# Maxima of the pooled scores of four heads in one reduction, with the last 32 queries scored in every row group

## The chip, the cores and the metric

One Trainium2 chip, one of its cores. The metric is the time of one execution in microseconds on the device, the median of several runs. The engines are TensorE (PE, with its weight loads as PEld), VectorE (DVE), ScalarE (ACT), GpSimd (POOL) and SyncE (SP, which here only issues transfers).

## What is computed

Attention over 4 batches, 8 heads, 576 positions of 64 numbers, then two mixer layers. The part around the change is the pooled attention:

```
q_d = q.reshape(B, H, Sd, factor, D).mean(axis=3)     # factor 4, Sd = 144; k_d, v_d alike
s = scale * q_d @ k_d^T;  s = s - max(s);  a = exp(s)
out_d = (a / (sum(a) + 1e-09)) @ v_d;  out_up = repeat(out_d, 4, axis=2)
...
x = out_up + out_local          # out_local: each position over its neighbours at |i - j| < 4
u = x + token mixing;  x = u + relu(u @ w_ch1) @ w_ch2;  then the second mixer (cos, sin)
```

Weights are given in 64-bit floats, q, k and v in 32-bit floats.

## The kernel before

The attention runs on **quads**: four heads of one batch, 8 quads in all, numbered 0 to 7 here in the order batch, half. Heads lie in two pairs (p) of two (j: partitions 0 to 63 and 64 to 127). For a quad `quad_front` adds four neighbours of q and k (`qa`, `qkd`, L343 and L344 on DVE), scores the pooled queries against the pooled keys on PE into the PSUM tile `sd` (L362 for the first 128 queries of each head, 32 rows at a time; L371 for the last 32, head 2j + p in row group 2j + p), takes the row maxima into `mxd` on DVE (L379 for the four blocks of 144 in all rows, L387 twice for the last 32 queries in 64 rows each), scales them (L389), exponentiates on ACT (`pd`, L394 and L399), transposes on PE (`pdt`, L403 and L408), copies on ACT (`pts`), multiplies with the values on PE (`od`, L417 to L425), divides on DVE (`ods`, L431) and writes the result to DRAM (L437, L440) to read it back repeated (`xu`, L443 and L446).

`pair_local` does the neighbour attention of one pair: scores `s` (L469, L471), maximum and difference on DVE (`mx` L482, `pbuf` L483), exp, transposes `pt` (L496), product `o` (L504), division on DVE (L512 to L515), and on POOL the sum with the pooled result, x = x + xu (L523). `token_mix` takes a quad's x through two products with hi and lo halves (`t`; `xl` L533, `h` L548, transposes L569). `channel_mix` of batch 0 uses `uh`/`ul` (L102), first products `c` by `mm3` (L105 to L107) with `g` (L237 on ACT, L238 on DVE), second products L247 to L250, and the sum `um` (L252 on DVE) that frees one of two PSUM banks.

Beside that, 64-bit weights are loaded (`raw`, L119, four buffers) and split (`converted`): ACT L127 and L129, a clamp on POOL (L130, every fifth of the first on DVE), DVE L135, L143, L148, L155, ACT L157, POOL L158, and a last sum L160. Up to about 260 us this is interleaved with attention and mixing; afterwards the channel layers of the remaining batches and the second mixer run, almost all of it PE work.

The order of the first stage comes in two steps. The table `ORDER` sets the order in which the program writes its steps (F a step of a quad, L of a pair, T of token mixing, C channel mixing, W, X and Y weights, P and V loads). A scheduler then places each instruction on its engine by its own estimate of when its inputs are ready. So a changed instruction can change the order of others on every engine. Each engine, and SP's issues, then run strictly in the order so fixed.

Of the kernel before, what the change touches and what calls it, by code (L numbers as in the profile page):

```python
# [12 lines left out]
F32 = mybir.dt.float32  # L13
# [5 lines left out]
AF = mybir.ActivationFunctionType  # L19
ALU = mybir.AluOpType  # L20
AX = mybir.AxisListType
# [20 lines left out]
SD = S // 4  # L42
# [20 lines left out]
def kernel(  # L63
# [19 lines left out]
    act, dve, pool, pe = nc.scalar, nc.vector, nc.gpsimd, nc.tensor  # L83
# [171 lines left out]
    with ExitStack() as actx:  # L255
        sb1 = actx.enter_context(tc.tile_pool(name="a1", bufs=1))
        sb2 = actx.enter_context(tc.tile_pool(name="a2", bufs=2))
# [6 lines left out]
        def wide(tag, name):  # L264
            if tag == "s" and spare is not None:
                return spare.tile([128, 2, 512], F32, tag="sp", name=name)
            return big.tile([128, 2, 512], F32, tag="big", name=name)
# [64 lines left out]
        def quad_front(b, hh):  # L332

            at = f"{b}_{hh}"
# [3 lines left out]
            qd, kd = qkd[:, :, 0], qkd[:, :, 1]  # L338
            for p in range(2):
# [11 lines left out]
                out=vl,  # L351
                in0=vs[:, 4:5, :].to_broadcast([128, 4, 65]),
                in1=diag.unsqueeze(2).to_broadcast([128, 4, 65]),
                op=ALU.mult,
# [3 lines left out]
            sd = wide("sd", f"sd_{at}")  # L358
            for p in range(2):
                for c in range(4):  # L360
                    for j in range(2):
                        pe.matmul(  # L362
                            sd[32 * c : 32 * c + 32, j, p * SD : (p + 1) * SD],
                            qd[64 * j : 64 * j + 64, p, 32 * c : 32 * c + 32],
                            kd[64 * j : 64 * j + 64, p, :],
                            start=True,
                            stop=True,
                        )
                for j in range(2):
                    c = 2 * j + p  # L370
                    pe.matmul(  # L371
                        sd[32 * c : 32 * c + 32, j, 2 * SD : 3 * SD],
                        qd[64 * j : 64 * j + 64, p, SD - 32 : SD],
                        kd[64 * j : 64 * j + 64, p, :],
                        start=True,
                        stop=True,
                    )
            mx = sb2.tile([128, 5], F32, tag="mxd", name=f"mxd_{at}")
            dve.tensor_reduce(  # L379
                out=mx[:, 0:4].rearrange("p (j a) -> p j a", j=2),  # L380
                in_=sd[:, :, 0 : 2 * SD].rearrange("p j (a n) -> p j a n", a=2),
                axis=AX.X,
                op=ALU.max,
            )
            for j in range(2):
                r = slice(64 * j, 64 * j + 64)
                dve.tensor_reduce(out=mx[r, 4:5], in_=sd[r, j, 2 * SD : 3 * SD], axis=AX.X, op=ALU.max)  # L387
            scale = 1.0 / (16.0 * math.sqrt(D))
            dve.tensor_scalar(out=mx, in0=mx, scalar1=-scale, scalar2=None, op0=ALU.mult)  # L389
            pd = sb1.tile([128, 5, SD], F32, tag="pd", name=f"pd_{at}")  # L390
            for j in range(2):
                for p in range(2):
                    i = 2 * j + p
                    act.activation(  # L394
                        pd[:, i, :], sd[:, j, p * SD : (p + 1) * SD], AF.Exp, scale=scale, bias=mx[:, i : i + 1]
                    )
            for j in range(2):
                r = slice(64 * j, 64 * j + 64)
                act.activation(pd[r, 4, :], sd[r, j, 2 * SD : 3 * SD], AF.Exp, scale=scale, bias=mx[r, 4:5])  # L399
            yield  # L400
            pt = wide("pd", f"pdt_{at}")
            for i in range(5):
# [2 lines left out]
            for o, i in ((128, 0), (256, 4)):  # L405
                for c in range(4):
                    out = pt[32 * c : 32 * c + 32, 1, o : o + 128]
# [184 lines left out]

        pairs = [(b, p4) for b in range(B) for p4 in range(4)]
        fronts = [quad_front(b, hh) for b in range(B) for hh in range(2)]
        locals_ = [pair_local(*p) for p in pairs]
        tokens = {}
# [213 lines left out]
    sb2 = ctx.enter_context(tc.tile_pool(name="c2p", bufs=2))  # L810
    op = ctx.enter_context(tc.tile_pool(name="op", bufs=3))
# [171 lines left out]
```

## Time and profile before

| | us |
|---|---|
| median of 3 runs | 760.28 (759.94 to 762.93) |
| profiled execution | 763.31, of which the span is 761.5 |
| PE busy | 713.3 |
| DVE busy | 475.8 |
| ACT busy | 316.7 |
| POOL busy | 264.9 |

The table covers the whole span, which has two parts of different kind, so the shares of the span say little; the views by stretch do. A row of a timeline gives the start, the duration, the engine, the line and the operation (written tile <- read tiles), and in brackets how long the engine had stood idle before it and what ended that.

### The profile page before, as it was taken

The numbers are of one execution on the slowest core, as the hardware profiler recorded it, in microseconds if no ns is written. First come the engines' busy times: TensorE is split into PE (matmuls) and PEld (weight loads), VectorE is DVE, ScalarE is ACT, GpSimd is POOL, SyncE is SP. The second block draws the span as 40 slices with busy tenths as digits, with TensorE's granted clock in tenths as the row PEclk, the third lists the DMA queues.
The fourth block names the chain that finished last, engine by engine and source line by source line (L and its number), as shares of the span: only waits on it lengthen the run. The fifth ranks groups of instructions, "written<-read, shape, count | busy, mean of one in ns | idle before, by whom it ended". The sixth has DMA issues, their size and how long they took to land.

```text
span 761.5 us, 19905 instructions
## 1 busy us (share of the span) xinstructions
PE 713.3 (94%) x8272; PEld 679.0 (89%) x8272; DVE 475.8 (62%) x1007; ACT 316.7 (42%) x756; POOL 264.9 (35%) x280
## 2 busy tenths in 40 slices
PE   6776968779999999999999999999999999999998
PEld 4555766678988899999999999999999999999998
DVE  3999999795345332489548866684674454554432
ACT  2654755643345322355234424352663353452310
POOL 1778788785111010177347746460000000000000
PEclk9776989979999999999999999999999999999999
DMA  9577584765544423558547857520000400300101
GB/s 286 176 235 200 180 279 129 247 207 164 191 127 127 126 88 124 195 178 260 194 149 230 281 188 254 192 77 32 32 1 2 132 1 1 125 1 2 63 1 64
DMA packets 58699, 105.50 MB, mean 139 GB/s; under 512 B 7920, under 2 KB 34672, under 8 KB 58608
## 3 DMA queue, kind: packets, MB, share of 16 engines
q1 hardware_dynamic: 58608, 104.22, 42.5%
q8 instruction: 65, 1.06, 0.6%
q14 instruction: 26, 0.21, 0.1%
HBM read 74.71 MB, written 29.49 MB: 137 GB/s over the span
## 4 chain that ended last, share of the span: by engine, by line
PE 73%; DVE 14%; DMA 5%; issue 3%; SPq 2%; POOL 1%; ACT 1%; DVEq 0%; POOLq 0%; ACTq 0%
PE c L105 6%; PE c L107 6%; PE c L106 6%; PE y L107 5%; PE y L105 5%; PE y L106 5%; PE c L724 5%; PE c L721 4%; PE c L720 4%; DVE ww L143 3%; PE th L105 2%; PE th L106 2%; PE th L107 2%; PE o L107 2%; PE o L105 2%
## 5 line engine op out<-in xcount | busy, mean ns | idle before, releaser
L130 POOL TENSOR_SCALAR ww<-ww 128x256 f32<-128x256 f32 (+1 forms) x85 | 99.7, 1175 | 117.5 <-ACT ww L129 88.7
L107 PE MATMUL y<-wrh,zl 128*128 128x288 f32 x256 | 75.7, 296 | 0.0
L106 PE MATMUL y<-wrl,zh 128*128 128x288 f32 x256 | 75.6, 295 | 0.0
L105 PE MATMUL y<-wrh,zh 128*128 128x288 f32 x256 | 75.6, 296 | 0.0
L707 ACT ACTIVATE g<-c 128x288 fp32r<-128x288 f32 x72 | 29.3, 412 | 90.6 <-PE c L107 90.6
L127 ACT ACTIVATE wf<-raw 128x256 bf16<-128x256 uint32 (+1 forms) x91 | 40.2, 442 | 38.8 <-DVE wrl L160 8.5
L143 DVE SCALAR_TENSOR_TENSOR ww<-raw,ww 128x256 uint32<-128x256 uint32 (+1 forms) x91 | 52.9, 583 | 2.2
L708 DVE SCALAR_TENSOR_TENSOR g<-c,g 128x288 fp32r<-128x288 f32 x72 | 32.3, 455 | 33.9 <-ACT g L707 33.4
L523 POOL TENSOR_TENSOR x<-x,xu 128x640 f32<-128x640 f32 x16 | 25.8, 1614 | 71.6 <-DVE x L515 40.4
L135 DVE TENSOR_SCALAR ww<-ww 128x256 uint32<-128x256 uint32 (+1 forms) x91 | 45.7, 504 | 4.2 <-POOL ww L130 4.0
L106 PEld LDWEIGHTS y<-wrl,zh 128*128 128x128 f32 x256 | 48.1, 188 | 0.0
L105 PEld LDWEIGHTS y<-wrh,zh 128*128 128x128 f32 x256 | 48.1, 188 | 0.0
L107 PEld LDWEIGHTS y<-wrh,zl 128*128 128x128 f32 x256 | 48.0, 188 | 0.0
L725 DVE TENSOR_TENSOR ut<-c,ut 128x288 f32<-128x288 f32 x48 | 21.9, 455 | 37.6 <-PE c L724 37.4
L148 DVE TENSOR_SCALAR we<-ww 128x256 uint16<-128x256 uint16 (+1 forms) x91 | 41.9, 462 | 0.7
L105 PE MATMUL th<-thh,cxh 128*128 128x256 f32 x144 | 41.1, 285 | 0.6 <-issue 0.6
L155 DVE TENSOR_TENSOR wf<-wf,we 128x256 bf16<-128x256 bf16 (+1 forms) x91 | 38.7, 426 | 3.5 <-ACT thh L157 0.5
L106 PE MATMUL th<-thl,cxh 128*128 128x256 f32 x144 | 40.7, 283 | 0.0
L107 PE MATMUL th<-thh,cxl 128*128 128x256 f32 x144 | 40.7, 283 | 0.0
L129 ACT ACTIVATE ww<-raw 128x256 f32<-128x256 f32 (+1 forms) x91 | 39.6, 435 | 0.0
L879 DVE TENSOR_TENSOR cx<-y,cx 128x288 f32<-128x288 f32 x32 | 14.6, 455 | 37.0 <-PE y L107 37.0
L106 PE MATMUL o<-cul,wch 128*128 128x288 f32 x128 | 37.4, 295 | 0.0
(285 smaller groups left out, 2468.8 us busy)
## 6 DMA issues: line engine op xcount, KB each, us to landing
raw<-w_ch SPq DMA_DIRECT2D x56, 256.0 KB, 3.3
qk<-qkT SPq DMA_DIRECT2D x16, 582.0 KB, 4.7
uh<-uh SPq DMA_DIRECT2D x16, 576.0 KB, 4.2
ul<-ul SPq DMA_DIRECT2D x16, 576.0 KB, 4.4
xT<-ut SPq DMA_DIRECT2D x14, 576.0 KB, 3.3
vw<-vloc SPq DMA_DIRECT2D x32, 219.4 KB, 4.2
vd<-vtok SPq DMA_DIRECT2D x8, 650.0 KB, 7.6
raw<-w_ri SPq DMA_DIRECT2D x18, 288.0 KB, 3.5
```

The costliest lines, as they stand in the source:

```text
L105: pe.matmul(out, lh, rh, start=start, stop=False)
L106: pe.matmul(out, lh, rl, start=False, stop=False)
L107: pe.matmul(out, ll, rh, start=False, stop=stop)
L127: act.activation(f, words[:, :, 0], AF.Copy, scale=2.0**-52)
L129: act.activation(w, high, AF.Abs)
L130: next(clamps).tensor_scalar(out=w, in0=w, scalar1=F64_LEAST, scalar2=F64_MOST, op0=ALU.max, op1=ALU.min)
L135: dve.tensor_scalar(out=wu, in0=wu, scalar1=3, scalar2=0x3FFFFFF8, op0=ALU.logical_shift_left, op1=ALU.bitwise_and,)
L143: dve.scalar_tensor_tensor(out=wu, in0=words[:, :, 1], scalar=0xC0000000, in1=wu, op0=ALU.bitwise_and, op1=ALU.bitwise_or)
L148: dve.tensor_scalar(out=e.bitcast(U16), in0=w.bitcast(U16).rearrange("p (n t) -> p n t", t=2)[:, :, 1], scalar1=0xFF80, scalar2=None, op0= ...
L155: dve.tensor_tensor(out=f, in0=f, in1=e, op=ALU.mult)
L708: dve.scalar_tensor_tensor(out=h2, in0=ps[:, 0:HALF], scalar=0.0, in1=h1.bitcast(F32), op0=ALU.max, op1=ALU.subtract)
L724: pe.matmul(ps[:, 0:HALF], w[cb // 2][2][:, cb % 2, d], hs[cb][1], start=False, stop=last_one)
```

## The change

The last 32 queries are scored in two row groups for each pair and half instead of one (L372: eight matmuls a quad instead of four), so that all 128 rows of the third block of `sd` hold scores of their half j. One reduction (L380) over both halves and three blocks gives six maxima a row in a tile of 2 x 3; it stands for three reductions. The scaling (L387) covers six columns instead of five, and the exponentials read their bias from the new places.

```diff
--- before.py
+++ after.py
@@ -366,37 +366,38 @@
                             start=True,
                             stop=True,
                         )
+
                 for j in range(2):
-                    c = 2 * j + p
-                    pe.matmul(
-                        sd[32 * c : 32 * c + 32, j, 2 * SD : 3 * SD],
-                        qd[64 * j : 64 * j + 64, p, SD - 32 : SD],
-                        kd[64 * j : 64 * j + 64, p, :],
-                        start=True,
-                        stop=True,
-                    )
-            mx = sb2.tile([128, 5], F32, tag="mxd", name=f"mxd_{at}")
+                    for c in (p, 2 + p):
+                        pe.matmul(
+                            sd[32 * c : 32 * c + 32, j, 2 * SD : 3 * SD],
+                            qd[64 * j : 64 * j + 64, p, SD - 32 : SD],
+                            kd[64 * j : 64 * j + 64, p, :],
+                            start=True,
+                            stop=True,
+                        )
+            mx = sb2.tile([128, 2, 3], F32, tag="mxd", name=f"mxd_{at}")
             dve.tensor_reduce(
-                out=mx[:, 0:4].rearrange("p (j a) -> p j a", j=2),
-                in_=sd[:, :, 0 : 2 * SD].rearrange("p j (a n) -> p j a n", a=2),
+                out=mx,
+                in_=sd[:, :, 0 : 3 * SD].rearrange("p j (a n) -> p j a n", a=3),
                 axis=AX.X,
                 op=ALU.max,
             )
-            for j in range(2):
-                r = slice(64 * j, 64 * j + 64)
-                dve.tensor_reduce(out=mx[r, 4:5], in_=sd[r, j, 2 * SD : 3 * SD], axis=AX.X, op=ALU.max)
             scale = 1.0 / (16.0 * math.sqrt(D))
             dve.tensor_scalar(out=mx, in0=mx, scalar1=-scale, scalar2=None, op0=ALU.mult)
             pd = sb1.tile([128, 5, SD], F32, tag="pd", name=f"pd_{at}")
             for j in range(2):
                 for p in range(2):
-                    i = 2 * j + p
                     act.activation(
-                        pd[:, i, :], sd[:, j, p * SD : (p + 1) * SD], AF.Exp, scale=scale, bias=mx[:, i : i + 1]
+                        pd[:, 2 * j + p, :],
+                        sd[:, j, p * SD : (p + 1) * SD],
+                        AF.Exp,
+                        scale=scale,
+                        bias=mx[:, j, p : p + 1],
                     )
             for j in range(2):
                 r = slice(64 * j, 64 * j + 64)
-                act.activation(pd[r, 4, :], sd[r, j, 2 * SD : 3 * SD], AF.Exp, scale=scale, bias=mx[r, 4:5])
+                act.activation(pd[r, 4, :], sd[r, j, 2 * SD : 3 * SD], AF.Exp, scale=scale, bias=mx[r, j, 2:3])
             yield
             pt = wide("pd", f"pdt_{at}")
             for i in range(5):
```

The number of instructions changes on PE (32 matmuls more) and on DVE (16 reductions fewer). The order changes on all engines in the first stage, up to row 3220 of PE's 6686 and row 419 of DVE's 1009; behind that it is the same.

On DVE, ahead of the `h` by which quad 3's token mixing passes from its first product to its second. Before:

```order
L515 TENSOR_TENSOR x_0_2694<-o_0_2650,rl_0_2691 128x2x5x64
L135 TENSOR_SCALAR ww<-ww 128x256
L252 TENSOR_TENSOR um_0_1166<-c_0_0_0_0_0_3049,um_0_1166 128x288
L143 SCALAR_TENSOR_TENSOR ww<-raw,ww 128x256
L148 TENSOR_SCALAR we<-ww 128x256
L252 TENSOR_TENSOR um_0_1166<-c_0_0_0_0_1_3069,um_0_1166 128x288
L155 TENSOR_TENSOR wf<-wf,we 128x256
L135 TENSOR_SCALAR ww<-ww 128x256
L143 SCALAR_TENSOR_TENSOR ww<-raw,ww 128x256
L548 SCALAR_TENSOR_TENSOR h_1_1_0_2559<-t_1_1_0_2543,h_1_1_0_2558 128x256
```

Now:

```order
L135 TENSOR_SCALAR ww<-ww 128x256
L102 TENSOR_TENSOR ul_0_1_0_3143<-um_1_1171,uh_0_1_0_3142 128x288 x2
L143 SCALAR_TENSOR_TENSOR ww<-raw,ww 128x256
L102 TENSOR_TENSOR ul_0_1_0_3143<-um_1_1171,uh_0_1_0_3142 128x288 x2
L148 TENSOR_SCALAR we<-ww 128x256
L483 TENSOR_REDUCE mx_2_2778<-s_2_2735 128x10
L155 TENSOR_TENSOR wf<-wf,we 128x256
L135 TENSOR_SCALAR ww<-ww 128x256
L484 TENSOR_TENSOR pbuf_133<-s_2_2735,mx_2_2778 128x2x5x38
L549 SCALAR_TENSOR_TENSOR h_1_1_0_2569<-t_1_1_0_2553,h_1_1_0_2568 128x256
```

The two sums into `um`, which stood ahead of this `h`, are now behind it; `mx` and `pbuf` of the tenth pair, which stood behind it, are now ahead.

On PE, from the end of quad 3's first product to the transposes that open its second (`t_1_1_0_0`). Before:

```order
L107 MATMUL t_1_1_1_2576<-xh_1_2536,w1l 128x256
L543 MATMUL t_1_1_1_2576<-xh_1_2536,w1h 128x256
L544 MATMUL t_1_1_1_2576<-xs_1_2538,w1s 128x256
L469 LDWEIGHTS id_132
L469 MATMUL s_2_2723<-msk,id_132 128x190
L469 LDWEIGHTS id_132
L469 MATMUL s_2_2723<-msk,id_132 128x190
L471 MATMUL s_2_2723<-qk_2_2325 32x38 x13
L569 MATMUL t_1_1_0_0_2596<-idt,x_1_2216 128x128 x2
L105 MATMUL t_1_1_0_0_2596<-w2h,h_1_1_0_2558 128x256
```

Now (`c` is the second product of batch 0's channel mixing):

```order
L250 MATMUL c_0_0_0_0_0_3061<-g_0_0_0_0_2_3007,c21h 128x288
L250 MATMUL c_0_0_0_0_0_3061<-g_0_0_0_0_3_3024,c21h 128x288
L250 MATMUL c_0_0_0_0_0_3061<-g_0_0_0_0_4_3041,c22h 128x288
L250 MATMUL c_0_0_0_0_0_3061<-g_0_0_0_0_5_3058,c22h 128x288
L247 MATMUL c_0_0_0_0_1_3081<-g_0_0_0_0_0_2972,c20h 128x288
L248 MATMUL c_0_0_0_0_1_3081<-g_0_0_0_0_0_2972,c20l 128x288
L247 MATMUL c_0_0_0_0_1_3081<-g_0_0_0_0_1_2989,c20h 128x288
L248 MATMUL c_0_0_0_0_1_3081<-g_0_0_0_0_1_2989,c20l 128x288
L570 MATMUL t_1_1_0_0_2606<-idt,x_1_2224 128x128 x2
L105 MATMUL t_1_1_0_0_2606<-w2h,h_1_1_0_2568 128x256
L106 MATMUL t_1_1_0_0_2606<-w2l,h_1_1_0_2568 128x256
```

In all, 14 second products of channel mixing that stood ahead of the transposes now stand behind them, and 27 score matmuls of the tenth pair and all 42 of the eleventh pair (40 and 2 of the mask) now stand ahead; the 13 shown before belong to the tenth pair as well.

On POOL, around the first sum of quad 3's x with its pooled result. Before:

```order
L130 TENSOR_SCALAR ww<-ww 128x256
L160 TENSOR_TENSOR c12l<-ww,wf 128x256
L158 TENSOR_TENSOR ww<-ww,c22h 128x256
L523 TENSOR_TENSOR x_1_2216<-x_1_2216,xu_1_2160 128x640
L160 TENSOR_TENSOR c22l<-ww,wf 128x256
L130 TENSOR_SCALAR ww<-ww 128x256
```

Now:

```order
L346 TENSOR_TENSOR vd_1_2572<-vd_1_2572 128x650
L160 TENSOR_TENSOR c12l<-ww,wf 128x256
L130 TENSOR_SCALAR ww<-ww 128x256
L158 TENSOR_TENSOR ww<-ww,c22h 128x256
L130 TENSOR_SCALAR ww<-ww 128x256
L160 TENSOR_TENSOR c22l<-ww,wf 128x256
L158 TENSOR_TENSOR ww<-ww,c22h 128x256
L524 TENSOR_TENSOR x_1_2224<-x_1_2224,xu_1_2168 128x640
L130 TENSOR_SCALAR ww<-ww 128x256
```

The sum with `xu` now has ahead of it one clamp (`ww<-ww` L130), one `c22l`, one subtraction (L158) and one `vd` sum that stood behind it.

## Rows read from the trace of the kernel before

**Rows 1.** Busy us of each engine by stretch, count in brackets, granted clock, DMA.
```profile
core 0: us, PE busy (x) PEld busy (x) DVE busy (x) ACT busy (x) POOL busy (x), PEclk, DMA share, GB/s
20.00:130.00 110.00, 84.61 (x1811) 67.54 (x1810) 105.31 (x220) 63.43 (x170) 87.12 (x92) 0.82 0.63 198
130.00:140.00 10.00, 7.82 (x144) 6.88 (x144) 6.21 (x17) 5.21 (x17) 6.24 (x8) 1.00 0.87 268
140.00:168.00 28.00, 20.11 (x381) 18.03 (x381) 27.47 (x54) 16.69 (x46) 24.79 (x26) 0.88 0.66 206
168.00:172.00 4.00, 4.00 (x40) 3.51 (x41) 2.50 (x7) 0.86 (x3) 2.31 (x3) 0.63 0.61 234
168.00:761.50 593.50, 587.01 (x5682) 577.40 (x5682) 328.53 (x704) 226.50 (x516) 142.88 (x149) 1.00 0.36 117
```

**Rows 2.** Timeline of PE: two long waits of the first stage.
```profile
103.05 0.61 PE L105 MATMUL c<-uh,c10h 128*128 128x288 f32 x1 [4.37 <-DVE pbuf L483]
...
167.94 0.44 PE L569 MATMUL t<-idt,x 128*128 128x128 f32 x2 [3.07 <-DVE h L548]
```

**Rows 3.** DVE by line and shape, 0 to 245 us: count, busy us, mean ns.
```profile
L135 DVE TENSOR_SCALAR ww<-ww 128x256 uint32<-128x256 uint32 x37 | 21.2, 578 | 4.1 <-POOL ww L130 4.0
L155 DVE TENSOR_TENSOR wf<-wf,we 128x256 bf16<-128x256 bf16 x37 | 19.5, 528 | 0.5
L148 DVE TENSOR_SCALAR we<-ww 128x256 uint16<-128x256 uint16 x37 | 15.9, 435 | 0.4
...
L482 DVE TENSOR_REDUCE mx<-s 128x10 f32<-128x380 f32 x14 | 7.6, 544 | 11.2 <-PE s L471 11.1
L483 DVE TENSOR_TENSOR pbuf<-s,mx 128x380 f32<-128x380 f32 x14 | 7.6, 543 | 0.2
L379 DVE TENSOR_REDUCE mxd<-sd 128x4 f32<-128x576 f32 x8 | 5.9, 744 | 0.6 <-PE sd L371 0.5
...
L387 DVE TENSOR_REDUCE mxd<-sd 64x1 f32<-64x144 f32 x16 | 4.8, 299 | 0.1
...
L252 DVE TENSOR_TENSOR um<-c,um 128x288 f32<-128x288 f32 x8 | 3.6, 451 | 7.8 <-PE c L250 7.8
```

**Rows 4.** Timeline of PE: from one group's start to the next one's.
```profile
12.70 0.48 PE L362 MATMUL sd<-qkd 64*32 64x144 f32 x16 [2.54 <-DVE qkd L344]
...
13.36 1.80 PE L282 MATMUL s<-zero 128*128 128x320 bf16 x12
...
43.67 0.33 PE L469 MATMUL s<-msk,id 128*128 128x190 bf16 x2
...
44.76 0.65 PE L417 MATMUL od<-vl,pts 128*32 128x260 f32 x8
...
179.17 0.29 PE L247 MATMUL c<-g,c20h 128*128 128x288 f32 x1
...
181.55 0.71 PE L496 MATMUL pt<-idt,pbuf 128*128 128x128 f32 x5
```

**Rows 5.** Timelines of POOL and DVE: the gap near 136 us.
```profile
136.44 1.55 POOL L523 TENSOR_TENSOR x<-x,xu 128x640 f32<-128x640 f32 x1 [3.76 <-DMA xu<-od]
...
138.59 1.06 POOL L130 TENSOR_SCALAR ww<-ww 128x256 f32<-128x256 f32 x1
...
139.68 0.82 DVE L135 TENSOR_SCALAR ww<-ww 128x256 uint32<-128x256 uint32 x1 [3.41 <-POOL ww L130]
```

**Rows 6.** POOL by line and shape, 100 to 168 us: count, busy us, mean ns.
```profile
L130 POOL TENSOR_SCALAR ww<-ww 128x256 f32<-128x256 f32 x14 | 17.0, 1215 | 2.3 <-ACT ww L129 2.3
...
L160 POOL TENSOR_TENSOR c22l<-ww,wf 128x256 fp32r<-128x256 f32 x4 | 3.4, 865 | 0.0
L158 POOL TENSOR_TENSOR ww<-ww,c22h 128x256 f32<-128x256 f32 x4 | 3.3, 836 | 0.0
...
L346 POOL TENSOR_TENSOR vd<-vd 128x650 f32<-128x650 f32 x2 | 2.8, 1392 | 0.5 <-DVE ww L143 0.5
```

**Rows 7.** Timeline of SP: the issue of the two `vw` loads.
```profile
132.04 0.58 SPq L457 DMA_DIRECT2D vw<-vloc  x1
132.66 0.43 SPq L458 DMA_DIRECT2D vw<-vloc  x1
```

## Prediction

> **What bounds the kernel now.** I read the busy time by stretch first, because the shares of the whole span hide two regimes [rows 1]. From 168 us to the end PE is busy 587.01 of 593.50 us: there the kernel is as long as PE's work. Before that PE is busy only 84.61 + 7.82 + 20.11 of 148 us, so 35.5 us of PE are lost, and in the same stretches DVE is busy 105.31 of 110 and 27.47 of 28 us. DVE, which runs its instructions in order, sets the pace up to 168 us, apart from ten microseconds (130 to 140) where it is busy 6.21. The waits of PE say the same: its two long ones shown are 4.37 us ended by `pbuf` and 3.07 us ended by `h`, both DVE's [rows 2]. The second of these is the last long wait: at 167.94 PE opens the second product of quad 3's token mixing, and from there on it hardly stops. I take that point as the hinge. The end of the kernel is the moment at which DVE finishes this `h`, plus the PE work that stands behind the hinge in PE's order. A microsecond of DVE counts if it stands ahead of the `h`, a microsecond of PE counts if it stands behind the hinge; the rest lies in waits. The price of what the change removes is in [rows 3], of what it adds and moves on PE in [rows 4], and the hole in DVE's work near 136 us in [rows 5].
>
> **The change part by part.** *The reductions.* Per quad 744 + 2 x 299 = 1342 ns go [rows 3]. From 144 to 576 elements a row the reduction grows by 445 ns, 1.03 ns an element, which leaves 299 - 148 = 151 ns that each instruction costs whatever its size. The new one reads 864 elements: 864 x 1.03 + 151 = 1041 ns. It saves 0.30 us a quad, in effect the fixed part of two instructions, since the elements are as many as before (576 + 144 + 144). The ends: nothing saved, if it cost 1342, and 0.60 saved, if it cost the 744 of the present large one; I take 0.30, from the slope of the two rows. Six of the eight quads stand ahead of the `h`: -1.8 us (0 to -3.6).
>
> *The order on DVE ahead of the `h`.* Counting the instructions ahead of it before and now, apart from the reductions: two sums into `um` have gone behind it (2 x 451 ns = -0.9), and the tenth pair's `mx` and `pbuf` (544 + 543) and one more instruction each of L135, L148 and L155 (578 + 435 + 528) have come ahead: +2.63 [rows 3]. Together +1.7 us. The reductions' gain ahead of the hinge is thus nearly used up by what the scheduler put there: -0.1.
>
> *The order on PE behind the hinge.* Fourteen second products of channel mixing fall behind it. Eighteen of them take from 179.17 to 181.55, 0.132 us each, so +1.85. Score matmuls, 27 of the tenth pair and all 42 of the eleventh, have come ahead; a pair's 42 take from 43.67 to 44.76, so 69 are 1.79 us that no longer stand behind. Net +0.1 [rows 4].
>
> *The added matmuls.* Twenty records of `sd` (ten matmuls, two records each) take from 12.70 to 13.36, 0.033 us a record [rows 4]. Four matmuls more are eight records, 0.26 us a quad. Of the eight quads six stand ahead of the hinge, where PE has 35.5 us of waits to hide them; uncovered, they would cost 1.6 us. Two stand behind: +0.5 us (0 if they overlap with others, twice that at the lower clock). The reduction waits for `sd` as it did before; DVE's idle time ahead of it was 0.6 us in eight quads [rows 3], so the wait is rarely the last one.
>
> *The sixth column and the exponentials' bias* are at nothing: the scaling has one element more, the six exponentials are as many and as large, and ACT is busy 16.69 of 28 us in the last stretch ahead of the hinge [rows 1].
>
> *The gap near 136 us.* DVE stood idle 3.41 us because POOL's clamp came late, and the clamp was late because POOL, in order, stood 3.76 us at x = x + xu, whose transfer had not landed [rows 5]. In the new order one clamp, one `c22l`, one subtraction and one `vd` sum stand ahead of that sum: 1215 + 865 + 836 + 1392 ns = 4.3 us of work that POOL can do first [rows 6]. On SP two `vw` loads now go out ahead of the `xu` loads, which makes these later by 0.58 + 0.43 = 1.0 us [rows 7]. POOL's wait would be 3.76 - 4.3 + 1.0 = 0.5 us, and DVE gets a clamped block before it instead of after it. The full gain would be 3.4 us; it is nothing if the pulled-forward rows wait for their own inputs, which DVE itself delivers. I take -2.0, nearer the full gain, since `vd` needs no DVE and the clamp needs only a loaded block.
>
> The sum: -1.8 + 1.7 + 0.1 + 0.5 - 2.0 = -1.5 us on the profiled execution, whose span is 761.5 and time 763.31. That execution was 3.0 us above the median of 760.28; I apply the difference to the median: 758.8. Without the gap's gain the sum is +0.5, with all of it -2.9.
>
> Two rules of the Trainium skill bear on this. First, PE's clock: in the four microseconds behind the 3.07 us wait the granted clock is 0.63, so 1.2 GHz for most of them, against 2.4 GHz in nearly all that follows; that loses 4 x 0.37 = 1.5 us of PE [rows 1, 2]. The Trainium skill (TensorE: Matmul & The Clock Gate, Part 1) says that the throttled clock is PE's default and activity releases it; the trace agrees. By it, filling the wait would be worth more than the wait's end alone: PE now has most of `c`'s second product there, and the lost clock might come back, which makes a sum of -3.0 instead of -1.5; it is a part of the fast rival below. Second, POOL's clamp takes 1215 ns on average in a stretch where DVE is nearly always busy and 1.06 us at 138.59, when DVE waited [rows 5, 6]. The Trainium skill (GPSIMD Engine Reference, 1. Specifications) says that POOL shares its SBUF interfaces with DVE and that DVE instructions with two SBUF inputs contend with it. The removed reductions read PSUM, so by that rule taking them away gives POOL no relief, and the freed time fills with instructions that do contend. That speaks for the POOL rival.
>
> **The rivals.** *The gap stays* (the pulled-forward POOL rows wait in their turn): +0.5, so 760.8. For it: the gap is a chain over DMA, POOL and DVE, and only one link is mended. *POOL sets the pace* ahead of the hinge: it is busy 24.79 of 28 us there [rows 1]. Then neither the gap nor the -1.8 of the reductions counts: +2.3, so 762.6. Against it: DVE waited for a clamp only 4.1 us in 245 [rows 3], and most of that is the gap. *The filled hinge* (fast): the gap goes wholly, and PE, fed with `c` in place of the 3.07 us wait, keeps its clock: -0.1 + 0.1 + 0.5 - 3.4 - 1.5 = -4.4, so 755.9. Against it: PE work moved into a wait ahead of the hinge only helps where it isn't missed elsewhere. *A new PE wait behind the hinge* (slower): the sums into `um` free the two PSUM banks of channel mixing; they now stand behind the `h` among other DVE work, while 14 of the products that need them stand behind the hinge too. If PE, which follows strictly in order, reaches the next product before its bank is free, it waits. Its longest wait of the kind, a `c` held up by DVE, was 4.37 us [rows 2], and the half clock behind such a wait costs 1.5: -1.5 + 5.9 = +4.4, so 764.7. It decides if PE's waits between 168 and 190 us grow by more than 2 us. Against it: about ten microseconds of other PE work (`t` and scores) stand between.
>
> **How the numbers follow.** My forecast of 758.8 (its own range 756.9 to 760.8, from the gap's two ends) gets 0.45, the gap stays 0.15, POOL sets the pace 0.10, the filled hinge 0.15, a new wait 0.15. About 0.5% of 760.28, 3.8 us, is what a measurement of this kernel can tell from no change. Below 756.5 lie most of the filled hinge and a tail of the forecast, since the order changes on every engine and the sum prices only the differences around one hinge: 0.24. Above 764.1 lie most of the new wait, little of POOL's pace, and the like tail: 0.18. Between: 0.58. The range of 755.2 to 764.9 reaches to the fast and slow rivals and leaves out two in ten.
>
> **What would show it right or wrong.** The reduction's row should read about 1040 ns, eight times, and `sd`'s added records should leave PE's busy time behind the hinge longer by about half a microsecond. DVE's longest idle time between 130 and 145 us should be under 2 us, and POOL's wait for `xu` under 1.5. PE's last long wait should still end with an `h` of quad 3, near 166 to 167 us. The forecast is wrong if PE's last long wait has moved to another place, above all one behind 170 us, or if DVE's busy share ahead of 168 us has fallen below 90% outside the gap, since then the hinge was never DVE's to set.

## The result and the profile after

The changed kernel takes 770.53 us (four runs, 767.43 to 772.42) against 761.58 for the kernel before in the same session: 1.0107 times as long (95% interval 1.0080 to 1.0134). The forecast was 758.8. A profiled execution is one run out of a spread of several us: that of the changed kernel, 767.43, was its fastest, and that of the kernel before, 763.31, was slower than all four of its runs in that session. Spans therefore differ by 4.0 us where medians differ by 9.0. Here the ratios judge, and the traces only tell where.

The view by stretch after, columns as in [rows 1]:

```profile
20.00:130.00 110.00, 79.44 (x1771) 63.50 (x1772) 93.98 (x205) 59.88 (x161) 84.60 (x90) 0.84 0.67 201
130.00:140.00 10.00, 8.65 (x130) 7.06 (x129) 9.36 (x23) 5.96 (x19) 7.11 (x9) 0.67 0.70 220
140.00:168.00 28.00, 22.94 (x477) 20.15 (x476) 21.98 (x47) 17.05 (x47) 22.25 (x25) 0.80 0.59 160
168.00:172.00 4.00, 4.00 (x103) 3.43 (x103) 3.71 (x8) 2.07 (x7) 4.00 (x4) 0.93 0.97 276
168.00:765.50 597.50, 590.57 (x5694) 582.27 (x5693) 333.51 (x704) 226.67 (x519) 144.55 (x150) 1.00 0.36 118
```

DVE's column changes most. Ahead of 130 us it is idle 16.0 us instead of 4.7, and from 140 to 168 us 6.0 instead of 0.5. That is not the loss itself: PE's idle time from 20 to 168 us grows by only 1.5 us, from 35.5 to 37.0, and its granted clock is lower from 130 us on, 0.67 and 0.80 instead of 1.00 and 0.88. Behind 168 us PE lacks 6.9 us, as it lacked 6.5 before. The loss is ahead of the hinge.

The new reduction by line and shape, 0 to 250 us (count, busy us, mean ns), and the timeline of POOL and DVE around the old gap, which answers to [rows 5]:

```profile
L380 DVE TENSOR_REDUCE mxd<-sd 128x6 f32<-128x864 f32 x8 | 8.4, 1050 | 0.2 <-PE sd L372 0.2
```

```profile
140.84 1.54 POOL L524 TENSOR_TENSOR x<-x,xu 128x640 f32<-128x640 f32 x1 [0.29 <-ACT c22h L157]
...
141.14 0.55 DVE L483 TENSOR_REDUCE mx<-s 128x10 f32<-128x380 f32 x1 [1.57 <-PE s L472]
...
143.44 0.76 DVE L135 TENSOR_SCALAR ww<-ww 128x256 uint32<-128x256 uint32 x1 [1.16 <-POOL ww L130]
...
146.38 0.76 DVE L343 TENSOR_TENSOR qa<-qk 128x576 f32<-128x576 f32 x1 [1.30 <-DMA qk<-qkT]
```

The wait for `xu` is gone, as forecast, and three shorter waits of DVE, 4.0 us together, stand just behind. Quad 3's transposes, which waited 3.07 us at 167.94 [rows 2], now start without a wait, but at 174.01, six us later (PE's timeline):

```profile
161.82 0.50 PE L470 MATMUL s<-msk,id 128*128 128x190 bf16 x2 [2.17 <-DVE x L516]
...
174.01 0.38 PE L570 MATMUL t<-idt,x 128*128 128x128 f32 x2
```

From that point to the end of the span it is 591.5 us, against 593.6 before. So the hinge lost 6.1 us, and what stands behind it gained 2.1.

One place where four engines stand still one behind the other, in the timelines of POOL, ACT, DVE and PE after:

```profile
112.14 1.53 POOL L524 TENSOR_TENSOR x<-x,xu 128x640 f32<-128x640 f32 x1 [3.93 <-DVE we L148]
...
115.75 0.43 ACT L127 ACTIVATE wf<-raw 128x256 bf16<-128x256 uint32 x1 [4.04 <-POOL c21l L160]
...
116.97 0.46 DVE L238 SCALAR_TENSOR_TENSOR g<-c,g 128x288 fp32r<-128x288 f32 x1 [3.15 <-ACT g L237]
119.86 1.95 DVE L534 TENSOR_TENSOR xl<-x,xh 128x1280 fp32r<-128x1280 f32 x1 [2.43 <-ACT xh L533]
...
117.48 0.61 PE L105 MATMUL c<-uh,c11h 128*128 128x288 f32 x1 [3.18 <-DVE g L238]
```

POOL's sum of quad 2's x with `xu` stands early and waits, by the view for a row of DVE. Behind it in POOL's order are the weight rows that free ACT's next buffer; behind ACT's conversion is the `g` that DVE wants; and PE wants DVE's `g` for a free bank.

### The profile page after: what moved, and what is told of

Same layout as the page of the kernel before. It is cut to its first block, busy times and chain, and to the rows that moved or that the text cites. A ratio compares the mean times of both kernels' runs of the same rounds, so it can differ in the third digit from the quotient of the medians.

```text
span 765.5 us, 20014 instructions
## 1 busy us (share of the span) xinstructions
PE 715.8 (94%) x8336; PEld 682.4 (89%) x8336; DVE 466.5 (61%) x991; ACT 315.2 (41%) x756; POOL 262.7 (34%) x280
## 3 DMA queue, kind: packets, MB, share of 16 engines
q8 instruction: 65, 1.06, 0.6%
## 4 chain that ended last, share of the span: by engine, by line
PE 75%; DVE 8%; DMA 6%; POOL 4%; issue 3%; ACT 2%; SPq 1%; POOLq 0%; DVEq 0%; ACTq 0%
PE c L105 6%; PE c L107 6%; PE c L106 6%; PE y L107 5%; PE y L105 5%; PE y L106 5%; PE c L725 4%; PE c L722 4%; PE c L721 4%; DMA vw<-vloc 2%; PE th L105 2%; PE th L106 2%; PE th L107 2%; PE o L107 2%; PE o L105 2%
## 5 line engine op out<-in xcount | busy, mean ns | idle before, releaser
L130 POOL TENSOR_SCALAR ww<-ww 128x256 f32<-128x256 f32 (+1 forms) x85 | 99.1, 1169 | 115.7 <-ACT ww L129 89.5
L135 DVE TENSOR_SCALAR ww<-ww 128x256 uint32<-128x256 uint32 (+1 forms) x91 | 43.4, 478 | 7.9 <-POOL ww L130 7.7
L148 DVE TENSOR_SCALAR we<-ww 128x256 uint16<-128x256 uint16 (+1 forms) x91 | 41.7, 460 | 0.6
L107 PE MATMUL o<-cuh,wcl 128*128 128x288 f32 x128 | 37.4, 295 | 0.0
```

The costliest lines, as they stand in the source:

```text
L107: pe.matmul(out, ll, rh, start=False, stop=stop)
L130: next(clamps).tensor_scalar(out=w, in0=w, scalar1=F64_LEAST, scalar2=F64_MOST, op0=ALU.max, op1=ALU.min)
L135: dve.tensor_scalar(out=wu, in0=wu, scalar1=3, scalar2=0x3FFFFFF8, op0=ALU.logical_shift_left, op1=ALU.bitwise_and,)
L148: dve.tensor_scalar(out=e.bitcast(U16), in0=w.bitcast(U16).rearrange("p (n t) -> p n t", t=2)[:, :, 1], scalar1=0xFF80, scalar2=None, op0= ...
```

## The experiments

In most of them each engine is held to a list of instructions, by edges that fix the order of issue and make no instruction wait for another's end:

```diff
+    for text in RANKS.values():     # one list per engine
...
+        for earlier, later in zip(row, row[1:]):
+            tc.add_manual_dep(traced[int(later)], traced[int(earlier)].name, info, reason="order")
```

A "lag" is worked out from two traces: instruction by instruction the start minus the start in the kernel before, and of these the median over VectorE's rows that the kernel before begins in a given ten us. The table has each ratio to the kernel before, and VectorE's busy time between 113 and 130 us, a stretch that the experiments single out.

| kernel | ratio (95%) | DVE busy of 17 us |
|---|---|---|
| before | 1 | 16.90 |
| changed | 1.0107 (1.0080 to 1.0134) | 11.33 |
| e1 changed instructions, old order | 1.0045 (1.0025 to 1.0066) | 14.89 |
| e2 old instructions, new order | 1.0110 (1.0092 to 1.0128) | 11.68 |
| e3 added matmuls, own order | 1.0160 (1.0128 to 1.0192) | 15.65 |
| e4 one reduction, own order | 1.0196 (1.0165 to 1.0227) | 16.11 |
| e5 new order to 97 us, then old | 1.0042 (1.0023 to 1.0062) | 16.68 |
| e6 old order to 97 us, then new | 1.0106 (1.0079 to 1.0133) | 8.90 |
| e7 one GpSimd row later | 1.0095 (1.0069 to 1.0122) | 11.26 |
| e8 added matmuls, old order | 1.0055 (1.0036 to 1.0075) | 16.90 |
| e9 one reduction, old order | 0.9987 (0.9973 to 1.0001) | 16.86 |
| e10 new order, old in 97 to 128 us | 1.0067 (1.0046 to 1.0088) | 16.62 |
| e11 old order, new in 97 to 128 us | 1.0101 (1.0080 to 1.0121) | 6.56 |
| e12 tail scores made twice, old order | 1.0021 (1.0008 to 1.0034) | 16.68 |
| e13 chain undone in the changed kernel | 1.0105 (1.0069 to 1.0140) | 7.60 |
| e14 chain undone in e11 | 1.0100 (1.0072 to 1.0129) | 9.75 |
| e15 added matmuls, last two quads | 1.0003 (0.9985 to 1.0021) | 16.90 |
| e16 e14 with weight rows put back | 1.0129 (1.0100 to 1.0158) | 7.27 |
| e17 e11 with weight rows put back | 1.0138 (1.0109 to 1.0167) | 5.75 |
| e18 as e16, in the changed kernel | 1.0121 (1.0088 to 1.0153) | 6.19 |

**Order or instructions: e1 to e4.** e1 and e2 exchange the two kernels' lists. e3 is the diff's part on the matmuls alone. e4 keeps four tail matmuls and reads other scores instead:

```diff
-                in_=sd[:, :, 0 : 3 * SD].rearrange("p j (a n) -> p j a n", a=3),
+                in_=bass.AP(s2.tensor, s2.offset, [*s2.ap[:2], (SD // 2, 3), (1, SD)]),
```

e1: 

> The changed kernel's instructions, all of them, but on every engine (TensorE, VectorE, ScalarE, GpSimd, SyncE) held in the order in which the kernel before has them; the 32 added matmuls stand beside their siblings. Theory (the loss is the new order of the first stage, the instructions themselves cost nothing): about 760 us, 0.995 to 1.002 of the kernel before; VectorE busy again over 104 of the 110 us from 20 to 130. Rival 1 (the added matmuls, the longer reduction or the longer hold of the scores cost it): about 770 us, 1.008 to 1.013 of the kernel before, as the changed kernel itself.

e2: 

> The kernel before's instructions, all of them, held on every engine in the order of the changed kernel; the three reductions of a quad stand together where the one stood. Theory (order): about 770 to 772 us, 1.008 to 1.015 of the kernel before, VectorE idle for over 10 us between 20 and 130 us. Rival 1 (instructions): within 0.3% of the kernel before.

e3: 

> The kernel before with the added matmuls alone (the three reductions stay), the scheduler free. By its instructions it should cost 0 to 1 us. Rival 1, with the matmuls as the cause: 1.008 to 1.013. Theory (order): the scheduler makes a third order of it, so the time says what a new order is worth and nothing of the matmuls: anything from 757 to 772 us; VectorE's idle time from 20 to 130 us goes with the time.

e4: 

> The changed kernel without the added matmuls, the scheduler free: one reduction of the same 128x6 size reads three overlapping runs of 144 of the written scores (it leaves out the maxima of the last 32 queries and takes those of half of either run in their place; the softmax is the same up to rounding). Rival 2 (the one larger reduction is the cause): 1.008 to 1.013. Theory (order): a fourth order, 757 to 772 us, and the time goes with VectorE's idle time from 20 to 130 us.

e2 has none of the changed instructions and loses 1.1%, all that the changed kernel loses: the order suffices for the loss. Holding an order costs nothing that these runs show: e15, further down, has six of the eight quads as they were, in the old order held by hand, and comes out at 1.0003. e1 lies between the two theories, so the instructions are not free either. The two do not add up: 1.1% and 0.45% give 1.07%. e3 and e4 got orders of their own and lose more than the changed kernel, though each has half the change, and though in the old order neither half loses as much (e8, e9). Their VectorE is busy at 113 to 130 us, and from 20 to 130 us 100.56 and 103.17 us, against 93.98 in the changed kernel: the loss does not go with VectorE's idle time, as both expectations had it. Where they lose was not followed. Three new orders out of three were worse than the old one.

**Which stretch: e5, e6, e10, e11.** The edit is in the lists alone: one kernel's list up to a time, then what is left in the other's order.

e5: 

> The changed kernel's instructions; every engine follows the changed kernel's order for all that it has begun by 97 us, and for the rest the order of the kernel before. Theory P (the loss lies at 107 to 117 us of the changed kernel, where GpSimd's x += xu of quad 2 stands ahead of three weight rows and waits 3.9 us, and ScalarE, VectorE and TensorE wait behind it in turn): as the changed kernel's instructions in the old order, 1.002 to 1.007 of the kernel before, about 765 us. Rival Q (the loss lies at 42 to 57 us, where the sum over vd of quad 2 and qa stand early and wait for loads): as the changed kernel, 1.008 to 1.013, about 770 us.

e6: 

> The other way round: the order of the kernel before for all that it has begun by 97 us, the changed kernel's order for the rest. Theory P (107 to 117 us): as the changed kernel, 1.008 to 1.013, about 770 us. Rival Q (42 to 57 us): 1.002 to 1.007, about 765 us.

e10: 

> The changed kernel in its own order, but for one stretch: what the kernel before begins up to 128 us, and the changed kernel has not begun by 97 us, stands in the order of the kernel before; from there on the changed kernel's order again. Theory P2 (the order of 97 to 128 us alone is the loss of the order): 1.002 to 1.007, about 765 us, and VectorE's lag against the kernel before, 4 to 5 us at 120 to 130 us in the changed kernel, is under 2 us there. Rival R (the order behind 128 us costs as much): 1.006 to 1.013, 766 to 771 us.

e11: 

> The complement: the changed kernel's instructions in the order of the kernel before, but for the stretch of 97 to 128 us, which stands as in the changed kernel. Theory P2: 1.007 to 1.012, about 768 to 770 us, a lag of 4 us or more of VectorE at 120 to 130 us, as in the changed kernel. Rival R: 1.002 to 1.007, about 765 us.

e5 is no slower than e1, so the new order ahead of 97 us costs nothing, though VectorE idles much more in it. Windows of e5:

```profile
20.00:97.00 77.00, 55.74 (x1171) 42.39 (x1174) 64.52 (x143) 43.66 (x119) 57.71 (x61) 0.82 0.64 191
97.00:130.00 33.00, 24.83 (x626) 21.59 (x619) 30.75 (x66) 17.95 (x48) 28.66 (x31) 0.85 0.68 204
```

VectorE is idle 12.5 of 77 us there; in the kernel before, busy 73.75 in the same window, it is idle 3.3. Nine us of idle time, and at 120 to 130 us the lag is 1.4 us. That does not show nine us to spare. Of the 9.2 us that VectorE is busy less, eight rows fewer make up about 2.6 (an estimate from the rows' means); the rest is rows of the same kind that ran shorter. Two groups of VectorE's rows in these 77 us (count, busy us, mean ns), in the kernel before and in e5:

```profile
L143 DVE SCALAR_TENSOR_TENSOR ww<-raw,ww 128x256 uint32<-128x256 uint32 x17 | 12.6, 752 | 0.1
L344 DVE TENSOR_TENSOR qkd<-qa 128x288 f32<-128x288 f32 x4 | 3.2, 788 | 0.1
```

```profile
L143 DVE SCALAR_TENSOR_TENSOR ww<-raw,ww 128x256 uint32<-128x256 uint32 x17 | 9.2, 544 | 0.2
L344 DVE TENSOR_TENSOR qkd<-qa 128x288 f32<-128x288 f32 x4 | 1.9, 466 | 0.0
```

e6 has the whole loss (lag 0.3 us or less up to 110 us, 5.0 at 120 to 130), and e11 has it too with 31 us of the new order; in both, the 0.45% of the changed instructions are contained. e11's lag is 0.1 at 100 to 110 and 9.6 at 120 to 130. The window 113 to 130 us, in the kernel before, in the changed one, in e11 and in e10:

```profile
113.00:130.00 17.00, 13.27 (x322) 11.52 (x323) 16.90 (x34) 9.82 (x25) 15.26 (x15) 0.90 0.43 121
```

```profile
113.00:130.00 17.00, 11.19 (x258) 9.73 (x259) 11.33 (x23) 8.11 (x19) 16.03 (x18) 0.83 0.67 213
```

```profile
113.00:130.00 17.00, 8.56 (x243) 7.40 (x244) 6.56 (x15) 7.48 (x18) 13.22 (x15) 0.79 0.60 168
```

```profile
113.00:130.00 17.00, 12.58 (x283) 10.27 (x282) 16.62 (x30) 9.25 (x24) 15.94 (x16) 0.90 0.48 141
```

e10 cures the window, but its 1.0067 lies in the ranges of both theories, and its interval meets that of e1 as well as that of the changed kernel. Its lag goes from 1.5 to 4.5 us at 130 to 140 us. So theory P2 holds in that the new order of this stretch alone, with the changed instructions, loses as much as the whole (e11); that what follows 128 us in the new order loses as well (rival R) is what e10's lag suggests, in one trace, and the times don't decide it.

**Which rows of the stretch: e7, e13, e14, e16, e17, e18.** e7 moves one row of POOL's order, e13 and e14 rows on ACT and DVE besides:

```diff
+POOL L158 ww<-ww,c21h x2
+POOL L160 c21l<-ww,wf
 POOL L524 x<-x,xu
-POOL L158 ww<-ww,c21h x2
-POOL L160 c21l<-ww,wf
...
+ACT L237 g (first block); wf, ww of the next load; pts, plt; g (second block); wf, ww; xh
-ACT wf, ww of the next load; g (first block); wf, ww; xh; pts, plt; g (second block)
...
+DVE L343 qa; L135 ww; L238 g (second block); L143 ww; L534 xl
-DVE L534 xl; L343 qa; L135 ww; L238 g (second block); L143 ww
```

e7: 

> The changed kernel in its own order, with one instruction moved: GpSimd's first x += xu of quad 2 stands behind the two products and the first rest (w - high - ...) of the weight blocks that are behind it in the changed kernel, three rows later. Theory P: GpSimd goes on at once, ScalarE's wait of 4.0 us before 115.75 us, VectorE's of 3.15 before 116.97 and TensorE's of 3.2 before 117.48 shrink by 2 to 3 us each; 1.5 to 3 us off, about 767.5 to 769 us, 1.004 to 1.009 of the kernel before. Rival Q: no change, 1.008 to 1.013.

e13: 

> The changed kernel in its own order with a few rows moved, all between 107 and 125 us: GpSimd's first x += xu of quad 2 three rows later (as in e7); on ScalarE the first channel block's g ahead of the next weight load's conversion, and the next conversion and xh behind pts, plt and the second g; on VectorE xl behind the four rows that follow it. TensorE and SyncE as in the changed kernel. Theory C (four rows that stand early and wait at the head of their queues pass the wait on, GpSimd to ScalarE to VectorE to TensorE): half or more of the loss comes back, 1.002 to 1.007 of the kernel before, 763 to 767 us, and no wait of VectorE over 2 us is left from 105 to 125 us. Rival D (the stretch loses by TensorE's order or by loads, whatever these rows do): 1.008 to 1.013, as the changed kernel.

e14: 

> e11 (the old order but for 97 to 128 us, 1.0101) with the same rows moved. Theory C: 1.001 to 1.006, 762 to 766 us; VectorE's lag of 9.6 us at 120 to 130 us is under 4 us. Rival D: 1.008 to 1.012, as e11.

e7's interval holds both its theory's range and the changed kernel's; it decides nothing. e13 and e14 are as slow as the kernels that they started from, so undoing the chain gains nothing. The chain is gone, and DVE waits as long or longer at another row; what the chain costs by itself is therefore not shown. In e13, timelines of SP and DVE:

```profile
106.62 2.52 SPq L444 DMA_DIRECT2D xu<-od  x4
...
115.89 0.52 SPq L453 DMA_DIRECT2D qk<-qkT  x1
...
125.27 0.76 DVE L343 TENSOR_TENSOR qa<-qk 128x576 f32<-128x576 f32 x1 [9.03 <-DMA qk<-qkT]
```

In e14, POOL and DVE:

```profile
112.74 1.54 POOL L524 TENSOR_TENSOR x<-x,xu 128x640 f32<-128x640 f32 x1 [0.67 <-DMA xu<-od]
...
119.41 1.34 POOL L346 TENSOR_TENSOR vd<-vd 128x650 f32<-128x650 f32 x1 [1.71 <-DMA vd<-vtok]
...
121.34 2.09 POOL L130 TENSOR_SCALAR ww<-ww 128x256 f32<-128x256 f32 x2
...
122.44 0.47 DVE L135 TENSOR_SCALAR ww<-ww 128x256 uint32<-128x256 uint32 x1 [6.79 <-POOL ww L130]
```

e16 to e18 therefore put one weight block's rows back on ACT, POOL and DVE, and on SP the loads ahead of `xu`:

```diff
+SP L459 vw; L119 raw x2; L336 vd; L444, L447 xu x6
-SP L444, L447 xu x6; L459 vw; L119 raw; L336 vd; L119 raw
```

e16: 

> e14 (the old order but for 97 to 128 us, with the chain of early rows undone: 1.0100) and besides one weight block's rows put back to where the kernel before has them: ScalarE's wf and |w| of that block ahead of the high part of the block before it, GpSimd's clamp of it and the rest of the block two before it earlier, VectorE's four rows of it ahead of the next block's clamp and the quad's maxima; and SyncE's loads of vw, two raw weight blocks and vd ahead of the six loads of xu. TensorE keeps the changed kernel's order of the stretch. Theory W (the order loses by weight blocks and loads that slip behind the quad's rows, so that VectorE runs dry at 113 to 125 us): 1.002 to 1.007, 763 to 767 us, VectorE's lag at 120 to 130 us under 3 us, the loads of the two raw blocks at 106 to 108 us as in the kernel before. Rival T (TensorE's order in the stretch is it): 1.008 to 1.012, as e11 and e14.

e17: 

> e16 with the chain of early rows left as in the changed kernel (GpSimd's first x += xu still ahead of the second block's product, ScalarE's conversion ahead of g and xh, VectorE's xl ahead of qa); only the weight block's rows and the loads are back. Theory W alone: as e16, 1.002 to 1.007. If both are needed: 1.006 to 1.011.

e18: 

> The changed kernel in its own order with the rows of e16 moved (and the load of the third qk of quad 2's second half ahead of xu too, which in e13 came 19 us later than in the kernel before and stopped VectorE for 9 us). Theory W: 1.003 to 1.008, 764 to 768 us, at or under what the whole old order in that stretch gave (e10, 1.0067). Rival T: 1.009 to 1.013, 768.5 to 771.5 us, as the changed kernel.

Theory W falls in all three, and e17 lies above the ranges of both its readings. Where the loads go ahead, POOL waits for `xu`, with the next blocks' clamps behind it (e16, POOL and DVE):

```profile
115.70 1.55 POOL L524 TENSOR_TENSOR x<-x,xu 128x640 f32<-128x640 f32 x1 [3.77 <-DMA xu<-od]
...
121.93 3.20 POOL L130 TENSOR_SCALAR ww<-ww 128x256 f32<-128x256 f32 x3
...
123.04 0.47 DVE L135 TENSOR_SCALAR ww<-ww 128x256 uint32<-128x256 uint32 x1 [9.73 <-POOL ww L130]
```

Two things stay alike in every kernel that has the new order in this stretch, and were not tried by themselves: PE's order, and POOL's two sums with `xu` and its sum over `vd` ahead of the next clamp. Which of them is the cause stays open.

**The instructions in the old order: e8, e9, e12, e15.** e8 and e9 are e3's and e4's instructions in the old order. e12 and e15 change one line of e8:

```diff
-                    for c in (p, 2 + p):
+                    for c in (p, 2 + p) * 2:
```

```diff
-                    for c in (p, 2 + p):
+                    for c in (p, 2 + p) if b == 3 else (2 * j + p,):
```

e8: 

> The kernel before with the added matmuls alone, the three reductions kept, every engine in the order of the kernel before. What the changed instructions cost in the old order measured 1.0025 to 1.0066. If the added matmuls are it (16 instructions per four quads ahead of 168 us, 0.41 us of TensorE a quad, or the clock that they bring): 1.003 to 1.007, 764 to 767 us. If it is the larger reduction or what it lets run earlier: 0.998 to 1.002, 761 to 763 us.

e9: 

> The single reduction of 128x6 without the added matmuls (it reads three overlapping runs of 144 of the written scores; the softmax is the same up to rounding), every engine in the order of the kernel before. Theory M (the matmuls cost what e8 showed, 1.0036 to 1.0075; the reduction gives what the sum said, 0.30 us a quad): 0.995 to 1.000, 758 to 761.4 us. Rival J (any change of the instructions, however small, loses about 0.4% against this order, whatever it is): 1.003 to 1.006, 764 to 766 us.

e12: 

> As e8 (added matmuls alone, the old order), but each of the eight score products of the last 32 queries is made twice: 12 more instructions a quad than in the kernel before instead of 4. Theory M (TensorE's time for them is what e8 lost): the loss of e8 times three, 1.011 to 1.020, 770 to 776 us. Rival J (what was lost is not the work but any disturbance of this order): as e8, 1.003 to 1.008, 764 to 767 us.

e15: 

> As e8 (added matmuls alone, the old order), but only in the two quads whose scores come behind 200 us; the six quads ahead of the wait at 168 us are as in the kernel before. If what e8 lost (1.0036 to 1.0075) is in the six quads ahead: 0.999 to 1.002, 761 to 763 us. If it is behind, where TensorE has no idle time, two quads of 0.05 to 0.1 us of TensorE more each: 1.003 to 1.007.

e9 is 1.0 us faster than the kernel before (2.1 faster to 0.1 slower). It is 1.2% faster than the changed kernel and the best version found, but not certainly better than the kernel before. e8 loses 0.55%, and e15 shows that this comes from the six quads ahead of 168 us, where PE has idle time. e12 speaks against both theories: with 96 instructions more it loses less than e8 with 32, and the intervals do not meet. The traces tell a part of that. Up to 255 us PE stands idle about as long in the profiled runs of both, 42.5 us in e8 and 43.0 in e12, but the granted clock is 0.89 in e8 and 0.92 in e12 (PE busy and count, granted clock, DMA; e8, then e12):

```profile
0.00:255.00 255.00, 212.55 (x4278) 0.89 0.62 195
```

```profile
0.00:255.00 255.00, 212.01 (x4409) 0.92 0.62 195
```

Over their spans, 761.2 us at 0.964 and 760.8 us at 0.973, the two runs lose 27.4 and 20.5 us to the clock. These 6.9 us less pay for e12's 64 matmuls more, which are 4.2 us by the 0.033 us a record of [rows 4] (an estimate). Why the clock is higher in e12, and why e8 loses, stays open.

## Why the prediction was wrong

*The step that failed* is "the order on DVE ahead of the `h`": "together +1.7 us". It priced the few rows that had come ahead or gone behind, each at its mean duration, and took DVE's idle time and the durations of all other rows as fixed, since DVE was busy 105.31 of 110 us [rows 1]. With the reductions this made -0.1 us. What the traces have up to that `h`, from DVE's timeline and its windows (busy and count, clock, DMA), before and after:

```profile
167.47 0.41 DVE L548 SCALAR_TENSOR_TENSOR h<-t,h 128x256 fp32r<-128x256 f32 x1
...
0.00:167.47 167.47, 146.79 (x302) 0.86 0.69 214
```

```profile
171.57 0.41 DVE L549 SCALAR_TENSOR_TENSOR h<-t,h 128x256 fp32r<-128x256 f32 x1
...
0.00:171.57 171.57, 136.29 (x294) 0.84 0.69 208
```

The `h` starts 4.1 us later: DVE is idle 14.6 us more ahead of it (35.3 instead of 20.7) and busy 10.5 us less. `mx` and `pbuf` took the 0.54 us that the prediction gave them, but rows of one shape do not have one duration. Two groups in the same windows, before and after:

```profile
L344 DVE TENSOR_TENSOR qkd<-qa 128x288 f32<-128x288 f32 x13 | 10.2, 784 | 0.3
L148 DVE TENSOR_SCALAR we<-ww 128x288 uint16<-128x288 uint16 x4 | 3.1, 784 | 0.1
```

```profile
L344 DVE TENSOR_TENSOR qkd<-qa 128x288 f32<-128x288 f32 x13 | 6.1, 467 | 0.1
L148 DVE TENSOR_SCALAR we<-ww 128x288 uint16<-128x288 uint16 x4 | 1.2, 301 | 0.0
```

The prediction named two signs of its being wrong, and both came. DVE's share outside the gap is 85% and 79%, under 90%. And PE's last wait of over 2 us has moved: it is the 2.17 us at 161.82, ended by `x` (L516) and not by an `h` of quad 3.

*That the hinge is DVE's to set* was wrong as well. After, both rows of `h` are done by 173.03 us (171.57 and 172.62, 0.41 us each), and PE comes to the transposes at 174.01 without a wait. From 161.82 on it is busy with what its own order has ahead of them, at a mean clock of 0.72:

```profile
161.82:174.01 12.19, 12.19 (x214) 10.92 (x215) 9.95 (x20) 8.74 (x25) 9.55 (x9) 0.72 0.79 241
```

That loses 12.19 x 0.28 = 3.4 us to the clock, over half of the 6.1 us by which the hinge came later (an estimate from this row). DVE was the busiest engine up to the hinge, but a full row of busy time did not show that a microsecond of it is worth one at the end: e4 has a DVE that is busy 103.17 of the 110 us, and is the slowest kernel of all.

*The reductions* were right in their duration: 1050 ns against 1041. Alone in the old order they bring 1.0 us (e9), somewhere between 2.1 faster and 0.1 slower; the forecast of 1.8 for six quads lies just inside that.

*The added matmuls* were mis-sized, and at the wrong place. The term was +0.5 us, all of it from the two quads behind the hinge, with the six ahead hidden at nothing and 1.6 us if uncovered. Measured in the old order: 0.2 us for the two quads behind (1.1 faster to 1.6 slower, e15), and about 4 for all eight (e8). That is not the matmuls' own work: made three times over, they cost 1.6 us (e12).

*The gap near 136 us* closed as forecast: DVE is busy 9.36 of those ten us instead of 6.21, and POOL's wait for `xu` there is gone.

*The hinge* was filled, as in the fast rival: no wait, and full clock behind it. Windows after, the hinge at 174.01:

```profile
162.00:166.00 4.00, 4.00 (x88) 3.36 (x87) 2.23 (x3) 3.87 (x12) 3.26 (x3) 0.50 0.66 185
166.00:170.00 4.00, 4.00 (x58) 3.62 (x56) 4.00 (x9) 3.10 (x10) 2.28 (x2) 0.68 0.78 205
170.00:174.00 4.00, 4.00 (x72) 3.81 (x71) 3.71 (x9) 1.60 (x4) 3.82 (x5) 1.00 0.98 340
174.00:178.00 4.00, 4.00 (x36) 4.00 (x35) 3.97 (x9) 2.56 (x7) 2.51 (x4) 1.00 0.91 370
```

In the four us from the hinge on the clock is 1.00, where it was 0.63 [rows 1], and PE had been busy for 12 us before it. The Trainium skill (TensorE: Matmul & The Clock Gate, Part 1) has activity release the throttled clock; the trace agrees. The prediction had reckoned this at 1.5 us from the rows; from the hinge to the end it is 2.1 us less, in which the work that changed sides and the added matmuls are contained too. But the half clock only moved: it now stands at 162 to 170 us, behind the wait of 2.17 us at 161.82, ahead of the hinge, which itself came 6.1 us later.

*The slow rival* ended on the right side with the wrong mechanism. It put a new wait of PE behind the hinge; PE's idle time behind 168 us grew by 0.4 us. "The order changes on every engine and the sum prices only the differences around one hinge" stood in the prediction as a tail; it was the main thing.

## What to carry to other kernels

Where a scheduler makes the order, first test the edit with the old order held: here that shows a reduction worth about 1 us, not certainly more than nothing, while the order that came with the edit costs 1.1% with the old instructions too. A sum of busy times says nothing of such an order, not even on the engine that looks full, whose rows may be stretched by what runs beside them: list the rows that come early, ask of each what it waits for, and price what is queued behind it. And a chain of waits in a trace is only a suspect; taking this one away moved the wait to another row and gained nothing.

## What was not expected of the hardware

The time of one and the same program goes with the clock that TensorE was granted: e1's fastest run is 762.48 us at a mean granted clock of 0.968, its slowest 769.47 at 0.953; which of the two follows the other is not shown. e12, with three times the added matmuls, has 0.969 on average over its runs, e8 0.963, the kernel before 0.965 in both sessions. That fits e12's smaller loss and the 6.9 us of its profiled run.

VectorE's rows take longer beside GpSimd's work. Row by row in the traces of the two kernels, up to 170 us: the 27 `we` (L148) of 128x256 that no GpSimd row overlaps took 0.23 to 0.30 us, the 41 others 0.28 to 1.65; the nine `qkd` (L344) without one 0.45 to 0.46, the 17 others 0.44 to 1.59. The new reduction, which reads PSUM, took 1.04 to 1.06 us either way. So a share of busy time holds such stretching too, and it can fall without any work being taken away. What in GpSimd's rows does it was not tried.
